# Loading block 0's values in long rows and gathering them on TensorE, in a chunked attention followed by a ReGLU feed-forward

## The chip, the cores and the metric

The kernel runs on one core of one Trainium2 chip. The time is device microseconds of one execution. Before the change it is 238.22 us, the median of 8 runs (237.99 to 238.51). A lower time is better.

## The reference

Attention over chunks of 32 queries: each chunk sees 8 memory rows, the 16 tokens to its left, its own 32 and the 8 to its right. The output is laid out as 3072 tokens of 512 numbers and goes through a gated feed-forward layer (FFN). `q`, `k`, `v` are 4 batches x 8 heads x 768 tokens x 64 in float32.

```
for c in range(nc):                                   # chunk 32, left 16, right 8
    l_start, r_end = max(0, c*32 - 16), min(S, c*32 + 32 + 8)
    k_full = concatenate([mem_k, k[:, :, l_start:r_end]], axis=2)
    v_full = concatenate([mem_v, v[:, :, l_start:r_end]], axis=2)
    scores = (1 / sqrt(64)) * q_c @ k_full.T
    a = softmax(scores)
    out[:, :, c*32:c*32+32] = a @ v_full
x = out.transpose(0, 2, 1, 3).reshape(3072, 512)
y = (maximum(x @ w_gate, 0) * (x @ w_val)) @ w_out    # 512 -> 1536 -> 512
```

## The kernel before

**Blocks and windows.** The tokens are worked in 8 blocks of 384 (`TB`), two for each batch. A block has four windows (`NQ`) of 96 queries; a window needs the 8 memory rows and 120 tokens (`BAND`), together 128 keys, one for each partition. Masks in the scores (block 0) or a bias in the exponential cut a window down to what each chunk of 32 sees. The eight heads go in four pairs, since two heads of 64 fill 128 partitions.

**Blocks 0 and 1.** They have nothing to hide behind and take a quicker way to their keys. `q` and `k` load in long rows: a partition holds four neighbouring tokens of a head (`J = 4`, 256 numbers). TensorE turns them (`turn_pe`, L199): for each of the four places in a row, `rk` is the stationary operand and a matrix of ones and zeros, `sel`, the moving one; this picks the rows that each window needs and transposes them in one step. `sel` for one window has 32 columns, 2 for the rows with the memory's eight tokens and 30 for the band's 120 tokens. `ident` does the same for the queries. In block 0 the result is written with a stride of four, so that tokens stand in their natural order. `turn_copy` (L210 to L216) brings it to SBUF in half precision on VectorE (DVE), the queries of pair 0 on ScalarE (ACT). `step_s0` (L250, L242, L254) makes the scores: a matmul with `maskk` and `maskq` writes the mask, eight add the products, and ACT takes the exponential. `wide_d` (L285) sums the exponentials with a matmul of ones, and ACT makes the reciprocal through a logarithm and an exponential (L288, L289). `ones[:, 1]` is for window 0 of block 0, whose 16 leftmost tokens don't exist. `wide_v` (L297) multiplies with the values `vwins` and DVE multiplies with the reciprocal (L299) into `xT`, the FFN's input.

**Values.** `vwins[p]` holds, for each window, the 8 memory rows and 120 band tokens of the eight heads in their key order. For block 0 `load_band` (L142) fetches the band with four DMAs, one a window, in rows of 64 numbers; the memory's rows come through `mem32`, are narrowed by DVE to `mem16` (L469) and copied into each window (L470).

**Queues.** Converting loads are issued by GpSimd (POOL), one after the other: block 0's keys and queries of heads 2 and 3, of heads 4 to 7, `ident` and `sel` between them (`select`, L429), the band of values, then the FFN's weights in slices of 256 columns (`load_w`, L172). [...] The keys and queries of heads 0 and 1 come in float32 through SP and ACT (`kst`, `qst`).

**FFN.** For each of 12 units of 128 columns `ffn_unit` (L342) makes gate and value with four matmuls each, ACT the positive part (L348), DVE the product `gv` (L349); `out_unit` (L368) multiplies `gv` with `wo`. Units 0 and 1 of block 0 are open together and are fed in `chunk`s, one for each head pair as it comes; unit 2 uses a spare double bank. The order of every engine is that of the program text; nothing reorders it.

**PSUM.** There are eight banks: `xo` and `xs`, and six that are first three double buffers (`tps`, for turns and scores of block 0), then four single ones (`fps`) and one double one (`sps`). `wide_v` of block 0 uses `xo` for all four pairs.

Of the kernel before, what the change touches and what calls it, by code (L numbers as in the profile page):

```python
# [17 lines left out]
def kernel(  # L18
# [12 lines left out]
    nc = tc.nc  # L31
# [52 lines left out]
    qbds = [const.tile([128, NQ, HP, 2, QB], F16, name=f"qbd{p}") for p in range(2)]  # L84
    memk, memv = (const.tile([NMEM, B * H, D], F16, name=nm) for nm in ("memk", "memv"))
    mem32 = const.tile([NMEM, H, D], F32, name="mem32")
    mem16 = const.tile([NMEM, H, D], F16, name="mem16")
    ones = const.tile([128, 3, D], F16, name="ones")
    bias = const.tile([128, 3], F32, name="bias")
    maskk = const.tile([128, 128], F16, name="maskk")  # L90
# [27 lines left out]
                       half.tile([QR, H, J * D], F16, tag="q16", name="rq"))  # L118
        return rows[n]

    def load_rows_mem(dma, dst, n, h0, nh):
        src = bass.AP(tensor=mem_k.tensor, offset=mem_k[n // 2, h0, 0, 0].offset,
                      ap=[[J * D, 2], [NMEM * D, nh], [1, J * D]])
        dma(dst, src)

    def load_k(n, h0, nh):
        pool_dma(rows_of(n)[0][0:KR, h0:h0 + nh], k_rows(n, h0, nh))  # L127
# [8 lines left out]
    def load_band(n, src_t, dsts):  # L136
        b, p = divmod(n, 2)
        for i in range(NQ):
            m0, m1 = (16 if (p == 0 and i == 0) else 0), (112 if (p == 1 and i == NQ - 1) else BAND)
            src = bass.AP(tensor=src_t.tensor, offset=src_t[b, 0, TB * p + QB * i - 16 + m0, 0].offset,  # L140
                          ap=[[D, m1 - m0], [S * D, H], [1, D]])
            pool_dma(dsts[p][NMEM + m0:NMEM + m1, i, :, 0:D], src)  # L142
# [38 lines left out]
        return pools["f"].tile([128, 512], F32, tag="f", name=name)  # L181

    def turn_pe(n, hp):

        if n != 1:
            pool, tag = (pools["t"], "t") if n == 0 else (pools["s"], "sc")
            ps = pool.tile([128, 2, 512], F32, tag=tag, name="kq_ps")
            kps, qps = ps[:, 0], ps[:, 1, 0:TB]
        else:
            ps, kps, qps = None, bank("k_ps"), bank("q_ps")[:, 0:TB]  # L190
        turns[n, hp] = ps, kps, qps
        rk, rq = (t.rearrange("p h (j d) -> p h j d", j=J) for t in rows_of(n))
        sel = sels[n % 2].rearrange("p i t -> p (i t)")

        for t, dst, w in ((rk, kps, sel[0:KR + 2]), (rq, qps, ident[:QR, :QR])):
            steps = dst.rearrange("p (r j) -> p j r", j=J) if n == 0 else dst.rearrange("p (j r) -> p j r", j=J)
            for j in range(J):
                for hh in range(2):
                    nc.tensor.matmul(steps[D * hh:D * hh + D, j], lhsT=t[:, 2 * hp + hh, j], rhs=w,  # L199
                                     start=True, stop=True)  # L200

    def turn_copy(n, hp):
        if n not in kTs:
            kq = turned.tile([128, HP, 512 + TB], F16, tag="kq", name="kq")
            kTs[n] = kq[:, :, 0:512].rearrange("p a (i m) -> p i a m", i=NQ)
            qTs[n] = kq[:, :, 512:].rearrange("p a (i m) -> p i a m", i=NQ)
            turns[n] = kq
        ps, kps, qps = turns.pop((n, hp))
        if n == 0 and hp == 0:
            dve_copy(turns[n][:, hp, 0:512], kps)  # L210
            act_copy(turns[n][:, hp, 512:], qps)
        elif n == 0:
            dve_copy(turns[n][:, hp], ps.rearrange("p a c -> p (a c)")[:, 0:512 + TB])
        else:
            for src, dst in ((kps, turns[n][:, hp, 0:512]), (qps, turns[n][:, hp, 512:])):
                dve_copy(dst.rearrange("p (r j) -> p r j", j=J), src.rearrange("p (j r) -> p r j", j=J))  # L216
# [19 lines left out]
    def score_mms(n, hp, sc, start):  # L236

        kT, qT = kTs[n], qTs[n]
        for i in range(NQ):
            for hh in range(2):  # L240
                s = slice(D * hh, D * hh + D)
                nc.tensor.matmul(sc[:, hh, QB * i:QB * i + QB], lhsT=kT[s, i, hp, :], rhs=qT[s, i, hp, :],  # L242
                                 start=start, stop=start or i == NQ - 1)

    def step_s0(n, hp):
# [43 lines left out]
        nc.scalar.activation(rinv, rinv, ACT.Exp, scale=-1.0, bias=mln64)  # L289
        rinvs[n, hp] = rinv  # L290

    def wide_v(n, hp):
        ex = exs.pop((n, hp))
        xo_ = xs if n == 1 and hp % 2 else xo
        for i in range(NQ):
            for hh in range(2):
                nc.tensor.matmul(xo_[D * hh:D * hh + D, QB * i:QB * i + QB], lhsT=vwins[n][:, i, 2 * hp + hh, 0:D],  # L297
                                 rhs=ex[:, hh, i, :], start=True, stop=True)
        nc.vector.tensor_tensor(out=x_of(n)[:, hp, :], in0=xo_, in1=rinvs.pop((n, hp)), op=ALU.mult)  # L299
# [45 lines left out]
    def ffn_close(n):  # L345
        for (g_ps, v_ps), m in units[n]:
            gr = grpool.tile([128, TB], F16, name="gr")
            nc.scalar.activation(gr, g_ps, ACT.Relu)  # L348
            nc.vector.tensor_tensor(out=gvs[n][:, m, :], in0=v_ps, in1=gr, op=ALU.mult)  # L349
# [37 lines left out]
    def fill(count):  # L387
        for i in range(count):
            nc.tensor.matmul(xo, lhsT=filler[:, 0:128], rhs=filler[:, 0:TB], start=True, stop=True)
# [9 lines left out]
    def words(t):  # L399
        return t.bitcast(U32)  # L400

    zero(words(filler), 0)
    zero(words(ident), 0)
    zero(words(sels[0].rearrange("p i t -> p (i t)")), 0)


    zero(vwins[0][0:NMEM + 16, 0, :, 0:D], 0.0)

    zero(words(maskk), 0)
    zero(words(maskq), 0)  # L410
    for g in range(3):
        r = slice(32 * g, 32 * g + 1)
        if g > 0:
            zero(maskk[r, NMEM:NMEM + 32 * g], NEG)
        if g < 2:
            zero(maskk[r, NMEM + 32 * g + 56:128], NEG)
        zero(maskq[r, 32 * g:32 * g + 32], 1.0)

    zero(words(ones.rearrange("p a d -> p (a d)")), 0x3C003C00)
    zero(ones[0:NMEM + 16, 1], 0.0)  # L420
    zero(ones[0:NMEM, 1], 1.0)
    zero(ones[96:128, 2], 0.0)
    zero(ones[96:120, 2], 1.0)
    zero(mln64, -LN64)
# [3 lines left out]
    def select(ap, fill_with, base, pattern, mult, op=ALU.not_equal):  # L428
        nc.gpsimd.affine_select(out=ap, in_=ap, compare_op=op, fill=fill_with, base=base, pattern=pattern,  # L429
                                channel_multiplier=mult)  # L430

    def build_sel(p):

        s = sels[p]
        first_row = -6 if p == 0 else 10
        parts = [(0, NQ, 2, 32)] if p == 0 else [(0, NQ, 2, 30), (0, NQ - 1, 30, 32)]
        for i0, i1, t0, t1 in parts:
            select(s[:, i0:i1, t0:t1], 1.0, -first_row - t0, [[-24, i1 - i0], [-1, t1 - t0]], 1)
        select(s[:, :, 0:2], 1.0, -KR, [[0, NQ], [-1, 2]], 1)

    load_k(0, 2, 2)
    load_rows_mem(pool_dma, rows_of(0)[0][KR:KR + 2, 2:H], 0, 2, H - 2)
    load_q(0, 2, 2)
    load_k(0, 4, 4)
    select(ident, 1.0, 0, [[-1, 128]], 1)
    build_sel(0)
    load_q(0, 4, 4)
    load_band(0, v, vwins)
    load_w(0, 256)
    load_w(256, 512)  # L450

# [11 lines left out]


    with tc.tile_pool(name="tps", bufs=3, space=bass.MemoryType.PSUM) as pools["t"]:
        fill(10)
        dve_copy(rows_of(0)[0][0:KR + 2, 0:2], kst)
        act_copy(rows_of(0)[1][:, 0:2], qst)
        dve_copy(mem16, mem32)  # L469
        mem_values = [lambda i=i: dve_copy(vwins[0][0:NMEM, i, :, 0:D], mem16) for i in range(NQ)]  # L470
        mem_values[0]()
        turn_pe(0, 0)
        turn_copy(0, 0)
        turn_pe(0, 1)
        turn_copy(0, 1)
        step_s0(0, 0)
        for i in range(1, NQ):
            mem_values[i]()
        turn_pe(0, 2)
        turn_copy(0, 2)  # L480
        step_s0(0, 1)
        wide_d(0, 0)
        turn_pe(0, 3)
        turn_copy(0, 3)
        step_s0(0, 2)
        wide_d(0, 1)
        step_s0(0, 3)
    pools["f"] = ctx.enter_context(tc.tile_pool(name="fps", bufs=4, space=bass.MemoryType.PSUM))
    pools["s"] = ctx.enter_context(tc.tile_pool(name="sps", bufs=1, space=bass.MemoryType.PSUM))
    wide_v(0, 0)  # L490
    wide_d(0, 2)
    wide_v(0, 1)
    zero(vwins[1][96:128, NQ - 1, :, 0:D], 0.0)


# [8 lines left out]
    select(bias, NEG, NMEM + 55, [[32, 3]], -1, ALU.is_ge)  # L504
    load_w(768, 1024)
    for i in range(NQ):
        nc.gpsimd.tensor_copy(vwins[1][0:NMEM, i, :, 0:D], mem16)
    load_w(1024, 1280)

    ffn_open(0, (0, 1))  # L510
    wide_v(0, 2)
    wide_d(0, 3)
    chunk(0, 0)
    chunk(0, 1)
    wide_v(0, 3)
    chunk(0, 2)
    chunk(0, 3)
    ffn_close(0)
    zero(words(k16s[0][0:32, 0].rearrange("p h d -> p (h d)")), 0)
    zero(words(k16s[1][96:128, NQ - 1].rearrange("p h d -> p (h d)")), 0)  # L520
    load_band(1, v, vwins)
# [5 lines left out]
    load_rows(2, 4, 4)  # L527

    ffn_unit(0, 2, spare=True)
    ffn_unit(0, 3)  # L530
    for hp in range(2):
        turn_pe(1, hp)
        turn_copy(1, hp)
    step_s(1, 0)
    for hp in range(2, HP):
        turn_pe(1, hp)
# [13 lines left out]
    ffn_unit(0, 8)  # L550
    ffn_unit(0, 9)
    for hp in range(HP):
        wide_v(1, hp)
    one_words(0, 0, NMEM + 16, 0, 1, 0)
    one_words(0, 0, NMEM, 0, 1, ONE)
    ffn_unit(0, 10)
# [88 lines left out]
```

The softmax here doesn't subtract the row's maximum and nothing guards it: scores larger than these inputs give would overflow.

## Time and profile before

| | |
|---|---|
| median of 8 runs | 238.22 us |
| the profiled execution | 238.51 us |
| its span, from the first to the last instruction | 236.6 us |
| TensorE busy, 0 to 40 us | 32.2 us |
| TensorE busy, 40 to 230 us | 190.0 us |
| first FFN matmul on block 0 (`g`; `v`) | 16.17; 17.31 us |
| first exponential of block 1 | 25.27 us |

The profile is of one execution and shows for each engine when each instruction ran and what released it. PE is TensorE's matmuls, PEld its weight loads. [...] a row's duration is longer than the distance to the next row; the distance is what counts. A DMA is shown by its issue on the queue, and its landing is given as a delay from there. In the table of stages the last three columns are TensorE's granted clock, the busy share of the 16 DMA engines, which sums overlapping packets and so exceeds 1, and GB/s.

### The profile page before, as it was taken

Reading aid. Unit: us, or ns where it says so; the run is one execution under the profiler, and the core shown is the slowest. Engines: PE = TensorE matmul, PEld = TensorE weight load, DVE = VectorE, ACT = ScalarE, POOL = GpSimd, SP = SyncE. Lnnn points to the kernel's source line nnn. Section 1 sums busy time; section 2 is a strip of 40 time slices with the busy share of each in tenths; the row PEclk is TensorE's granted clock in tenths of the full one; section 3 lists DMA queues with packets and bytes.
Section 4 is the critical chain, followed back from the end, with each engine's and each line's share of the span. In section 5 each row is a group of like instructions: output and inputs, shape, how many; then the busy total and the mean of one; then the engine's idle time right before and its main releaser. Section 6 shows DMA issues by size and latency. Waiting matters only on the chain.

```text
span 236.6 us, 4591 instructions
## 1 busy us (share of the span) xinstructions
PE 225.0 (95%) x1730; PEld 131.2 (55%) x1730; DVE 107.2 (45%) x215; ACT 141.0 (60%) x299; POOL 104.1 (44%) x131
## 2 busy tenths in 40 slices
PE   6869888999999999999999999999999999999993
PEld 3535545566544566546664666556664666455641
DVE  5655727889710155604642156405561266214400
ACT  3393693377752589728883599548881798433310
POOL 7988967945307940893099205960310000000000
PEclk9999999999999999999999999999999999999999
DMA  6999999999994999299939993999702100120012
GB/s 121 137 166 194 196 173 182 166 206 155 92 200 150 147 161 169 22 153 201 164 20 163 148 148 53 98 180 171 79 3 89 44 3 0 44 91 0 1 46 89
DMA packets 107324, 27.35 MB, mean 116 GB/s; under 512 B 91222, under 2 KB 104358, under 8 KB 107302
## 3 DMA queue, kind: packets, MB, share of 16 engines
q0 software_dynamic: 83008, 15.37, 80.7%
q1 hardware_dynamic: 20630, 5.33, 18.8%
q10 hardware_dynamic: 3664, 6.36, 7.8%
q8 instruction: 13, 0.21, 0.4%
q14 instruction: 9, 0.07, 0.1%
HBM read 31.15 MB, written 6.29 MB: 158 GB/s over the span
## 4 chain that ended last, share of the span: by engine, by line
PE 85%; DMA 4%; POOL 3%; ACT 3%; issue 2%; DVE 2%; POOLq 0%; DVEq 0%; ACTq 0%
PE g_ps L342 26%; PE v_ps L342 25%; PE o_ps L368 25%; DMA wv<-in_moe_w_val_dram 3%; PE sc_ps L267 3%; PE xo_ps L306 2%; ACT ex L273 2%; PE xs_ps L306 2%; POOL vwin L142 2%; PE kq_ps L199 1%; DMA out_dram<-o_sb 1%; PE sc_ps L242 1%; POOL rk L127 1%; PE gv_ps L342 1%; ACT rw L288 0%
## 5 line engine op out<-in xcount | busy, mean ns | idle before, releaser
L349 DVE TENSOR_TENSOR gv<-v_ps,gr 128x384 f16<-128x384 f32 x95 | 52.8, 557 | 97.4 <-ACT gr L348 84.2
L342 PE MATMUL v_ps<-xT,wv 128*128 128x384 f16 x380 | 78.3, 326 | 0.8 <-DMA wv<-in_moe_w_val_dram 0.8
L342 PE MATMUL g_ps<-xT,wg 128*128 128x384 f16 x380 | 78.3, 326 | 0.0
L368 PE MATMUL o_ps<-wo,gv 128*128 128x512 f16 x288 | 63.5, 379 | 0.0
L348 ACT ACTIVATE gr<-g_ps 128x384 f16<-128x384 f32 x95 | 46.0, 485 | 22.0 <-PE g_ps L342 10.8
L342 PEld LDWEIGHTS <-wg 128*128 128x128 f16 x384 | 36.6, 98 | 22.7
L342 PEld LDWEIGHTS <-wv 128*128 128x128 f16 x384 | 36.2, 98 | 22.8 <-DMA wv<-in_moe_w_val_dram 1.0
L368 PEld LDWEIGHTS <-gv 128*128 128x128 f16 x288 | 28.0, 98 | 33.0
L230 POOL COPY qbd<-qT 64x1536 f16<-64x1536 f16 x10 | 14.6, 1462 | 55.9 <-DMA qT<-q16n 55.6
L377 ACT COPY o_sb<-o_ps 128x512 f32<-128x512 f32 x23 | 13.5, 586 | 39.0 <-PE o_ps L368 31.0
L273 ACT ACTIVATE ex<-sc_ps,bias 128x256 f16<-128x256 f32 x84 | 33.3, 466 | 3.9 <-PE sc_ps L242 3.2
L142 POOL DMA_DIRECT2D vwin<-in_v_dram x32 | 29.1, 936 | 1.5 <-DMA memv<-in_mem_v_dram 1.1
L315 ACT ACTIVATE rinv<-ln,mln 64x768 f32<-64x768 f32 x24 | 22.1, 923 | 0.0
L310 ACT ACTIVATE ln<-xo_ps 64x384 f32<-64x384 f32 x24 | 11.7, 487 | 16.3 <-PE xs_ps L306 16.3
L168 POOL DMA_DIRECT2D q16n<-in_q_dram x20 | 15.6, 803 | 5.6 <-DMA wo<-in_moe_w_out_dram 5.6
L142 POOL DMA_DIRECT2D k<-in_k_dram x20 | 17.9, 910 | 0.0
L321 DVE TENSOR_TENSOR xT<-xo_ps,rinv 64x384 f16<-64x384 f32 x24 | 13.1, 547 | 10.0 <-ACT rinv L315 9.9
L321 DVE TENSOR_TENSOR xT<-xs_ps,rinv 64x384 f16<-64x384 f32 x24 | 13.2, 550 | 0.7
L306 PEld LDWEIGHTS <-vwin 128*128 128x128 f16 x192 | 10.6, 98 | 3.0
L310 ACT ACTIVATE ln<-xs_ps 64x384 f32<-64x384 f32 x24 | 11.4, 474 | 0.0
L306 PE MATMUL xo_ps<-ex,vwin 128*128 128x96 f16 x96 | 11.1, 206 | 0.0
L306 PE MATMUL xs_ps<-ex,vwin 128*128 128x96 f16 x96 | 11.1, 206 | 0.0
(79 smaller groups left out, 133.9 us busy)
## 6 DMA issues: line engine op xcount, KB each, us to landing
out_dram<-o_sb ACTq DMA_DIRECT2D x23, 256.0 KB
vwin<-in_v_dram POOLq DMA_DIRECT2D x24, 120.0 KB, 7.3
q16n<-in_q_dram POOLq DMA_DIRECT2D x20, 96.0 KB, 5.4
k<-in_k_dram POOLq DMA_DIRECT2D x15, 120.0 KB, 4.1
wg<-in_moe_w_gate_dram POOLq DMA_DIRECT2D x6, 256.0 KB, 7.6
wv<-in_moe_w_val_dram POOLq DMA_DIRECT2D x6, 256.0 KB, 8.1
wo<-in_moe_w_out_dram POOLq DMA_DIRECT2D x3, 512.0 KB, 10.8
rk<-in_k_dram POOLq DMA_DIRECT2D x5, 224.0 KB, 6.4
```

The source lines that it names most:

```text
L142: pool_dma(dsts[p][NMEM + m0:NMEM + m1, i, :, 0:D], src)
L168: pool_dma(q16s[n][:, i], src)
L230: nc.gpsimd.tensor_copy(qbds[n % 2][s, :, :, hh, :].rearrange("p i a m -> p (i a) m"), qTs[n][s].rearrange("p i a m -> p (i a) m"))
L273: nc.scalar.activation(flat[:, :, :, s], view[:, :, :, s], ACT.Exp, scale=SCALE, bias=bias[:, g:g + 1])
L306: nc.tensor.matmul((xo, xs)[hh][:, QB * i:QB * i + QB], lhsT=vw[:, i, 2 * hp + hh, :], rhs=ex[:, hh, i, :], start=True, stop=True)
L310: nc.scalar.activation(ln[:, hh], (xo, xs)[hh][D:128], ACT.Ln, scale=1.0 / 64.0)
L315: nc.scalar.activation(rinv, lns.pop((n, hp)), ACT.Exp, scale=-1.0, bias=mln64[0:D, :])
L321: nc.vector.tensor_tensor(out=x_of(n)[D * hh:D * hh + D, hp, :], in0=(xo, xs)[hh][0:D], in1=rinv[:, hh, :], op=ALU.mult)
L342: nc.tensor.matmul(ps[a], lhsT=(wg, wv)[a][:, f, 128 * m:128 * m + 128], rhs=xTs[n][:, f, :], start=(f == 0), stop=(f == NFC - 1))
L348: nc.scalar.activation(gr, g_ps, ACT.Relu)
L349: nc.vector.tensor_tensor(out=gvs[n][:, m, :], in0=v_ps, in1=gr, op=ALU.mult)
L368: nc.tensor.matmul(o_ps, lhsT=gvs[n][:, m, 128 * t:128 * t + 128], rhs=wo[:, m, :], start=(m == 0), stop=(m == NDC - 1))
```

## The change

Block 0's values come in long rows as its keys do: one DMA for 112 rows of 256 numbers for each head, and one for the memory's two rows, into a new tile `rv`. TensorE distributes them: `gather_v(i0)` makes, for two windows at a time, eight matmuls with `sel`'s 32 columns as stationary operand and `rv` at place `j` of the row as moving one; place `j` goes to the partitions 32 j to 32 j + 31. DVE copies the result, 128 x 1024, into `vwins[0]`. The keys of block 0 therefore stand by their place in the row: key 32 j + t is row t's token j. `turn_pe` writes them so, `maskk` is laid out so, and `ones[:, 1]` is made by four matmuls with `sel`.

Beside this: `ident` and `sel` are cleared by POOL and built before POOL's loads; the queries of pair 0 go through `xs` to a tile of their own, `q00`; the scores of pair 1 come ahead of the turn of pair 2; `wide_v` of pairs 1 and 3 uses a second double bank, `xo2`; the sums of pairs 2 and 3 are at other places; the turns of pairs 0 and 1 of block 1 come ahead of unit 3; clearing a part of `vwins[0]` moves from the start to after unit 1; one more filler matmul; `mem16` goes.

```diff
-        for t, dst, w in ((rk, kps, sel[0:KR + 2]), (rq, qps, ident[:QR, :QR])):
-            steps = dst.rearrange("p (r j) -> p j r", j=J) if n == 0 else dst.rearrange("p (j r) -> p j r", j=J)
+        ksteps, qsteps = (dst.rearrange("p (j r) -> p j r", j=J) for dst in (kps, qps))
+        if n == 0:
+            ksteps = kps.rearrange("p (i j t) -> p j i t", i=NQ, j=J)
+            qsteps = qps.rearrange("p (r j) -> p j r", j=J)
+        for t, steps, w in ((rk, ksteps, sel[0:KR + 2]), (rq, qsteps, ident[:QR, :QR])):
...
         if n == 0 and hp == 0:
             dve_copy(turns[n][:, hp, 0:512], kps)
-            act_copy(turns[n][:, hp, 512:], qps)
+            act_copy(q00, qps)
...
-    def wide_v(n, hp):
+    def wide_v(n, hp, xo_=xo):
...
-    zero(words(ident), 0)
-    zero(words(sels[0].rearrange("p i t -> p (i t)")), 0)
-    zero(vwins[0][0:NMEM + 16, 0, :, 0:D], 0.0)
...
+        keys = maskk[r].rearrange("p (j t) -> p j t", j=J)
         if g > 0:
-            zero(maskk[r, NMEM:NMEM + 32 * g], NEG)
+            zero(keys[:, :, 2:2 + 8 * g], NEG)
...
-    zero(ones[0:NMEM + 16, 1], 0.0)
-    zero(ones[0:NMEM, 1], 1.0)
...
+    nc.gpsimd.memset(words(ident), 0)
+    nc.gpsimd.memset(words(sels[0].rearrange("p i t -> p (i t)")), 0)
+    select(ident, 1.0, 0, [[-1, 128]], 1)
+    build_sel(0)
     load_k(0, 2, 2)
...
     load_k(0, 4, 4)
-    select(ident, 1.0, 0, [[-1, 128]], 1)
-    build_sel(0)
     load_q(0, 4, 4)
-    load_band(0, v, vwins)
+    pool_dma(rv[0:KR], bass.AP(tensor=v.tensor, offset=v[0, 0, 0, 0].offset,
+                               ap=[[J * D, KR], [S * D, H], [1, J * D]]))
+    load_rows_mem(pool_dma, rv[KR:KR + 2], 0, 0, H, mem_v)
     load_w(0, 256)
...
+        def gather_v(i0):
+
+            ps = pools["t"].tile([128, 2, 512], F32, tag="t", name="vg_ps")
+            for i in range(2):
+                for j in range(J):
+                    nc.tensor.matmul(ps[32 * j:32 * j + 32, i].rearrange("p (h d) -> p h d", h=H),
+                                     lhsT=sels[0][0:KR + 2, i0 + i, :], rhs=rv[:, :, D * j:D * j + D],
+                                     start=True, stop=True)
+            dve_copy(vwins[0][:, i0:i0 + 2, :, 0:D].rearrange("p i h d -> p (i h) d"),
+                     ps.rearrange("p i (h d) -> p (i h) d", h=H))
+
+        fill(11)
+
+        for j in range(J):
+            nc.tensor.matmul(xo[32 * j:32 * j + 32, 0:D], lhsT=sels[0][0:KR + 2, 0, :], rhs=ones[0:KR + 2, 0, :],
+                             start=True, stop=True)
...
-        dve_copy(mem16, mem32)
-        mem_values = [lambda i=i: dve_copy(vwins[0][0:NMEM, i, :, 0:D], mem16) for i in range(NQ)]
-        mem_values[0]()
+        dve_copy(ones[:, 1], xo[:, 0:D])
...
         step_s0(0, 0)
-        for i in range(1, NQ):
-            mem_values[i]()
+        step_s0(0, 1)
         turn_pe(0, 2)
         turn_copy(0, 2)
-        step_s0(0, 1)
         wide_d(0, 0)
...
         step_s0(0, 3)
+        gather_v(0)
+        wide_d(0, 2)
+        gather_v(2)
...
+    xo2 = pools["s"].tile([128, 2, 512], F32, tag="sc", name="xo2_ps")
     wide_v(0, 0)
-    wide_d(0, 2)
-    wide_v(0, 1)
+    wide_v(0, 1, xo2[:, 0, 0:TB])
...
     ffn_open(0, (0, 1))
+    wide_d(0, 3)
     wide_v(0, 2)
-    wide_d(0, 3)
     chunk(0, 0)
     chunk(0, 1)
-    wide_v(0, 3)
+    wide_v(0, 3, xo2[:, 1, 0:TB])
     chunk(0, 2)
     chunk(0, 3)
     ffn_close(0)
+
+    zero(vwins[0][0:NMEM + 16, 0, :, 0:D], 0.0)
...
     ffn_unit(0, 2, spare=True)
-    ffn_unit(0, 3)
     for hp in range(2):
         turn_pe(1, hp)
         turn_copy(1, hp)
+    ffn_unit(0, 3)
     step_s(1, 0)
```

More of the change, by code (lines that the diff above doesn't have):

```diff
@@ L86 @@
     mem32 = const.tile([NMEM, H, D], F32, name="mem32")
-    mem16 = const.tile([NMEM, H, D], F16, name="mem16")
+    rv = const.tile([KR + 2, H, J * D], F16, name="rv")
+    q00 = const.tile([128, TB], F16, name="q00")
     ones = const.tile([128, 3, D], F16, name="ones")
@@ L119, in rows_of, with load_rows_mem @@
         return rows[n]
-    def load_rows_mem(dma, dst, n, h0, nh):
-        src = bass.AP(tensor=mem_k.tensor, offset=mem_k[n // 2, h0, 0, 0].offset,
+    def load_rows_mem(dma, dst, n, h0, nh, src_t=mem_k):
+        src = bass.AP(tensor=src_t.tensor, offset=src_t[n // 2, h0, 0, 0].offset,
                       ap=[[J * D, 2], [NMEM * D, nh], [1, J * D]])
@@ L187, in turn_pe @@
             ps = pool.tile([128, 2, 512], F32, tag=tag, name="kq_ps")
-            kps, qps = ps[:, 0], ps[:, 1, 0:TB]
+            kps, qps = ps[:, 0], xs if (n, hp) == (0, 0) else ps[:, 1, 0:TB]
         else:
@@ L241, in score_mms @@
                 s = slice(D * hh, D * hh + D)
-                nc.tensor.matmul(sc[:, hh, QB * i:QB * i + QB], lhsT=kT[s, i, hp, :], rhs=qT[s, i, hp, :],
+                rhs = q00[s, QB * i:QB * i + QB] if (n, hp) == (0, 0) else qT[s, i, hp, :]
+                nc.tensor.matmul(sc[:, hh, QB * i:QB * i + QB], lhsT=kT[s, i, hp, :], rhs=rhs,
                                  start=start, stop=start or i == NQ - 1)
@@ L290, in wide_d @@
         rinvs[n, hp] = rinv
-    def wide_v(n, hp):
+    def wide_v(n, hp, xo_=xo):
         ex = exs.pop((n, hp))
-        xo_ = xs if n == 1 and hp % 2 else xo
         for i in range(NQ):
@@ L412 @@
         r = slice(32 * g, 32 * g + 1)
+        keys = maskk[r].rearrange("p (j t) -> p j t", j=J)
         if g > 0:
-            zero(maskk[r, NMEM:NMEM + 32 * g], NEG)
+            zero(keys[:, :, 2:2 + 8 * g], NEG)
         if g < 2:
-            zero(maskk[r, NMEM + 32 * g + 56:128], NEG)
+            zero(keys[:, :, 2 + 8 * g + 14:32], NEG)
         zero(maskq[r, 32 * g:32 * g + 32], 1.0)
     zero(words(ones.rearrange("p a d -> p (a d)")), 0x3C003C00)
-    zero(ones[0:NMEM + 16, 1], 0.0)
-    zero(ones[0:NMEM, 1], 1.0)
     zero(ones[96:128, 2], 0.0)
@@ L465 @@
     with tc.tile_pool(name="tps", bufs=3, space=bass.MemoryType.PSUM) as pools["t"]:
-        fill(10)
+        def gather_v(i0):
[11 more added lines that the diff above has]
+                             start=True, stop=True)
         dve_copy(rows_of(0)[0][0:KR + 2, 0:2], kst)
         act_copy(rows_of(0)[1][:, 0:2], qst)
-        dve_copy(mem16, mem32)
-        mem_values = [lambda i=i: dve_copy(vwins[0][0:NMEM, i, :, 0:D], mem16) for i in range(NQ)]
-        mem_values[0]()
+        dve_copy(ones[:, 1], xo[:, 0:D])
         turn_pe(0, 0)
@@ L506 @@
     for i in range(NQ):
-        nc.gpsimd.tensor_copy(vwins[1][0:NMEM, i, :, 0:D], mem16)
+        nc.gpsimd.tensor_copy(vwins[1][0:NMEM, i, :, 0:D], mem32)
     load_w(1024, 1280)
     ffn_open(0, (0, 1))
+    wide_d(0, 3)
     wide_v(0, 2)
-    wide_d(0, 3)
     chunk(0, 0)
     chunk(0, 1)
-    wide_v(0, 3)
+    wide_v(0, 3, xo2[:, 1, 0:TB])
     chunk(0, 2)
@@ L552 @@
     for hp in range(HP):
-        wide_v(1, hp)
+        wide_v(1, hp, (xo, xs)[hp % 2])
     one_words(0, 0, NMEM + 16, 0, 1, 0)
```

## The prediction, made before the changed kernel ran

> **What bounds the kernel now.** I read the page's busy shares, then the busy time by stage, then what TensorE waited for, then the chain of waits of the first 50 us, last single rows of the timeline.
>
> ```profile
> span 236.6 us, 4591 instructions
> PE 225.0 (95%) x1730; PEld 131.2 (55%) x1730; DVE 107.2 (45%) x215; ACT 141.0 (60%) x299; POOL 104.1 (44%) x131
> ```
>
> ```profile
> 5.00:10.00 5.00, 3.49 (x58) 2.57 (x57) 3.31 (x7) 1.45 (x3) 5.00 (x7) 1.00 1.36 130
> 10.00:15.00 5.00, 4.63 (x78) 2.63 (x75) 2.74 (x3) 4.03 (x7) 5.00 (x10) 1.00 1.67 150
> 15.00:20.00 5.00, 3.49 (x35) 1.87 (x35) 1.95 (x4) 2.31 (x6) 3.46 (x7) 1.00 1.40 184
> 40.00:230.00 190.00, 190.00 (x1332) 110.93 (x1331) 84.33 (x155) 117.56 (x252) 70.60 (x76) 1.00 1.03 106
> ```
>
> The columns of the second fence are stage, length, then busy us of PE, PEld, DVE, ACT, POOL. From 40 us to 230 us TensorE is never idle, so nothing there can be won by this change: the time is decided by how early TensorE enters that stage. What the first 40 us leave idle is named by the waits (engine, line, releaser, us in total, times, longest):
>
> ```profile
> PE xo_ps L297 <- DVE xT L299: 1.8, 3, 0.7
> PE kq_ps L199 <- DMA rq<-in_q_dram: 0.8, 1, 0.8
> PE kq_ps L199 <- POOL sel L429: 0.8, 1, 0.8
> PE v_ps L342 <- DMA wv<-in_moe_w_val_dram: 0.8, 1, 0.8
> PE sc_ps L242 <- DVE kq L216: 0.7, 1, 0.7
> ```
>
> The chain (start, us, what) shows which of them ends last:
>
> ```profile
> 5.98 3.71 POOL vwin L142 x4
> ...
> 10.47 6.79 DMA wv<-in_moe_w_val_dram
> 17.26 0.05 issue
> 17.31 0.34 PE v_ps L342
> ...
> 23.15 0.56 DVE gv L349
> 23.71 1.07 DVE kq L216 x2
> 24.78 0.04 issue
> 24.82 0.36 PE sc_ps L242 x8
> 25.22 0.05 issue
> 25.27 1.21 ACT ex L273 x3
> ```
>
> The reader is to see two things. First, four issues of the value load keep POOL for 3.71 us ahead of the weights, and the FFN's first `v` matmul waits until 17.31 for them, though attention's first output was ready at about 14.6. Second, the FFN's work leads through unit 3's product and two copies to block 1's first exponentials at 25.27; from there ACT sets the pace until TensorE is full at 33.6 us. So I reckon the start of those exponentials: its shift is the shift of the end.
>
> ```profile
> 9.64 0.52 PE L199 MATMUL kq_ps<-ident,rq 96*64 96x96 f16 x8 [0.83 <-DMA rq<-in_q_dram]
> ...
> 10.20 1.09 DVE L213 CAST kq<-kq_ps 128x896 f16<-128x896 f32 x1 [0.98 <-PE kq_ps L199]
> ...
> 11.96 1.09 DVE L213 CAST kq<-kq_ps 128x896 f16<-128x896 f32 x1 [0.67 <-PE kq_ps L199]
> ```
>
> These rows show the other path that counts: heads 4 to 7 of block 0's queries land, TensorE turns them, DVE copies twice 1.09 us.
>
> [...] The trace has no 32-column matmul[...]: eight of 96 columns at L297 let the next row begin 0.16 us later (13.55 to 13.71). [...] 512 columns in 0.69 us and 896 in 1.09 make 1.04 ns a column. [...] 135 GB/s between 9 and 11 us, where the packets are the values' 128 B, 178 to 196 GB/s from 13 to 20 us with 512 B packets. [...] POOL's selections would now stand beside DVE's memsets, in the trace they stand beside two casts, so I price them as they are.
>
> **The change, part by part.** Times below are on the clock of the profile.
>
> *POOL.* Now: four DMA issues from 1.35, the three selections 4.26 to 5.33, queries of heads 4 to 7 issued at 5.28, values 5.97 to 9.69, weights from 9.68. After: two memsets and the selections come first. POOL may start at about 0.8 (SP and ACT issue at 0.80). A memset of 64 words isn't in the trace for POOL; its memsets of one column last 0.10, DVE's of 64 words 0.11; I take 0.1 each, 0.3 at most, not below nothing since DVE's own come free only in slack. With 0.1 for waits and 1.07 for the selections, the first load is issued at 2.2 (bound 2.6) instead of 1.35. Then 0.82 + 0.61 + 0.67 + 0.75 put the last query load at 5.05, against 5.28. The value load: four issues of 0.93 (3.72) become one, priced as the nearest row of 120 x 8 rows (0.93), and one of 0.62 for the memory's two rows: the weights are issued at 7.3 instead of 9.68.
>
> *Landing.* Keys of heads 4 to 7 took 4.8 us from issue, queries 4.3, landing 1.39 after each other. Issued at 4.3 and 5.05: by its own delay the query load lands at 9.35, behind the keys with the old distance at 10.5. I take 9.85 (before 9.58). Both ends go into the range. The first turns also wait: pair 1's queries land at 3.63 + 3.3 = 6.9 instead of 6.07, but the scores of pair 1 now come ahead of the turn of pair 2, so this lies beside the same wait and costs nothing unless the late load comes sooner.
>
> *Values.* 459 kB of 512 B packets at 178 GB/s: 2.6 us, landed at 12.45; at 135 GB/s 3.4, at 13.25. Then the four weight loads at 1.35 each (17.26, 18.61, 19.95 landed at this distance): the first `wv` at about 15.2. The 0.8 us wait for it goes; what is late next is the gather.
>
> *Attention's front.* Queries at 9.85, first copy 0.56 later: 10.41 to 11.5, second to 12.6. Now the scores of pair 3 follow that copy's end by 0.23 (13.05 to 13.28) and take 0.28: the gather starts at 13.1, after its rows have landed. It is 2 x 8 matmuls of 512 columns. o_ps shows 0.216 each (54 in 11.65), in fours beside each other 0.43 for eight, alone 1.73; I take 0.43, plus 0.2 until DVE may start. DVE's copies are 1024 columns: 1.04 x 1024 + 0.16 = 1.22 each. First 13.75 to 14.97, second to 16.2; TensorE's second half of the gather hides under the first copy. Then the second half of wide_v and the product: 16.6 to 17.16. wide_v of pair 2 must wait for it (same bank), then 0.29: `g` begins at 17.5. Now `v` begins at 17.31 with one `g` already done. From 17.31 to wide_v of pair 3 it is 1.24 for seven matmuls, so 1.40 for eight; from there to unit 2 1.73 (18.55 to 20.28). Unit 2 begins at 20.63 instead of 20.28: **0.35 later**. The second bank for pairs 1 and 3 removes two of the three L297 waits, but they lay before the weights' landing and are paid again by the copies.
>
> *Units 2 and 3 and the turns.* Unit 3 moves behind two turns. Now unit 2 starts t = 20.28 and the exponentials t + 4.99. After: unit 2's product can start at t + 2.02 as now (22.30), but a third memset of 0.27 stands before it in DVE's queue; the two there already end 0.14 before the product, and each needs 0.36 with its gap. So the product is 0.24 late. Then 0.56, k copy 0.68, q copy 0.55 (t + 4.05); unit 3 must wait for them, as its two banks are those just turned into; its `v` ends at about t + 4.85 and the exponentials begin at t + 5.25. The 0.7 us wait of the scores at L242 is not won, it becomes a wait of unit 3: **0.25 later**. Queued behind unit 3's `g` are the scores of pair 0, and ACT waits for those.
>
> *At nothing:* copying the query turn to its own tile by ACT, mask memsets in 3-d, the extra fill, the four matmuls and the copy for the ones (all before 5.9, under the wait for the loads; without it 0.3 to 0.5, from 64 columns at 1.04 ns with their fixed part and four short matmuls); unstrided key writes, perhaps 0.1 a turn, under DVE's copies; the value memory's rows no longer copied by DVE (0.51 and four of 0.27, 1.6 us in all, which lay beside waits of DVE for TensorE).
>
> **Sum:** 0.35 + 0.25 = 0.6. The profiled execution is 238.51 us (span 236.6 and 1.9 around it), so 239.1; it was the slowest of eight whose median is 238.22. Against the median: **238.8 us**.
>
> **The rivals.** *Early loads (not slower).* Now the late keys and queries are issued on either side of the selections; after, in one run. If the last queries land with the 3.3 to 3.4 us that the small loads need instead of 4.3 to 4.8, at 8.4 to 9.2, then everything from DVE's first copy to unit 2 is 0.65 to 1.5 earlier; at 8.85 this is 1.0, so 237.8. It decides from a landing at 9.25 (238.2). For it: between 7 and 8 us the DMA engines moved only 94 GB/s. Against it: keys now start 0.9 later and the queries follow them on the same queue. *Gather one by one (slower).* If four column groups don't run together, DVE's second copy starts 1.73 + 0.28 + 1.73 + 0.2 = 3.94 after the gather's begin instead of 1.89: 2.05 more, 240.9. Against it: the 64-column rows. *Rows late (slower; the change doesn't do what it says).* If the long rows go no faster than the short, they land 13.25 to 14.1, and TensorE waits in the gather: 0.2 to 1.0 more, 239.5 at 0.7. Against it: the 178 to 196 GB/s.
>
> **How the numbers follow.** Forecast 0.43 (own range 238.3 to 239.3), early loads 0.32, one by one 0.10, rows late 0.15. A measurement of this kernel tells 0.2% (0.48 us) from no change. Faster comes from three quarters of the early loads: 0.24. Within 0.2%: the rest of these, 0.08, and 0.16 of the forecast's low part: 0.24. Slower: 0.27 of the forecast and both slow rivals: 0.52. The range, 237.4 to 240.1, leaves out the lowest part of the early loads and the one-by-one case. The likeliest case gives the time.
>
> **What would show it.** Right: the last query load lands at 9.4 to 10.5; no wait for `wv`; a TensorE wait for the copies of vg_ps of 1.5 us or more before wide_v; two copies of about 1.22; unit 3's `g` waiting for the kq copies; the exponentials of block 1 beginning 0.3 to 1.0 after 25.27. Wrong: queries landed by 9.25; copies well under 1.1; eight gather matmuls taking over 1 us; TensorE falling back to 0.33 us for 384 columns, as its fillers at the start show, in the idle stretch before the FFN.

## The result, and the profile after

The changed kernel takes 241.04 us in the median of 11 executions (239.23 to 242.06), the kernel before 238.24 (31 executions beside it, 237.77 to 239.03). The ratio is 1.0111, 95% interval 1.0095 to 1.0127: slower, and by more than the range of the prediction allowed. The profiled execution took 241.49 us with a span of 239.3, so 2.2 us lie around it.

The head of the page, and TensorE's clock in 40 slices:

```profile
span 239.3 us, 4626 instructions
PE 228.1 (95%) x1751; PEld 131.7 (55%) x1751; DVE 107.7 (45%) x209; ACT 141.2 (59%) x299; POOL 101.6 (42%) x131
...
PEclk9797999999999999999999999999999999999999
```

TensorE is busy for 3.1 us more than before (228.1 against 225.0), though the gather adds only sixteen matmuls in two groups of 0.6 us. The last row says why: the second and the fourth slice stand at 7 tenths. Between the two, and after them, the clock is full. Cut at the places where the clock changes, the stages look like this (stage, length, busy us of PE, PEld, DVE, ACT and POOL with their instructions, then the granted clock, the DMA share and GB/s):

```profile
4.17:7.58 3.41, 2.21 (x39) 1.32 (x37) 1.35 (x3) 1.10 (x2) 3.41 (x6) 1.00 1.12 132
7.58:10.99 3.41, 3.41 (x42) 1.72 (x38) 1.09 (x1) 1.58 (x2) 3.41 (x8) 0.50 1.26 152
10.99:14.40 3.41, 3.37 (x62) 1.78 (x58) 2.10 (x3) 2.68 (x6) 1.52 (x3) 1.00 1.41 185
14.40:17.82 3.42, 1.67 (x34) 0.72 (x33) 2.98 (x4) 2.33 (x5) 2.15 (x4) 1.00 1.44 191
17.82:21.23 3.41, 3.41 (x24) 1.66 (x23) 1.23 (x3) 0.74 (x2) 3.18 (x8) 0.50 1.45 195
21.23:24.60 3.37, 3.37 (x38) 1.94 (x36) 2.11 (x5) 1.18 (x3) 3.37 (x6) 1.00 1.45 196
```

Two stretches of 3.41 us run at half clock, and each follows a stretch of the same length in which TensorE stood idle for a good part: it was busy for 2.21 us of 3.41 ahead of the first, 1.67 of 3.42 ahead of the second, where its longest wait was 0.86. The two half-clock stretches were full (3.41 busy), and the full clock follows each of them. The clock changes at 7.58, 10.99, 17.82 and 21.23 us and falls again at 239.68, behind the last instruction. The distances are 3.41, 6.83, 3.41 and 218.45 us: 1, 2, 1 and 64 steps of 3.413. In the profile of the kernel before the clock stays full from 4.39 us to 236.5, after TensorE's last matmul, which is 232.11 us or 68 such steps. Counted back from that fall in these steps, the emptiest of its stretches up to 230 us is this one:

```profile
14.63:18.04 3.41, 1.89 (x26) 1.11 (x26) 1.39 (x3) 2.68 (x5) 2.53 (x4) 1.00 1.38 178
```

1.89 us busy kept the clock there; 1.67 and 2.21 lost it here. The count depends on where a stretch is taken to begin: from 13.95 to 17.36, off these steps, TensorE of the kernel before is busy for only 1.53 us, and the clock stayed. With 1.89 us, between the two, the kernel before is close to losing it too.

The waits of TensorE in the first 42 us (what waited, for what; us in total, times, longest) show what took the place of the wait for `wv`, which is gone:

```profile
PE xo_ps L301 <- DVE vwin L476: 1.4, 2, 0.9
...
PE xo_ps L301 <- DVE xT L303: 1.1, 2, 0.7
PE g_ps L346 <- DVE kq L220: 1.0, 1, 1.0
PE kq_ps L203 <- DMA rq<-in_q_dram: 1.0, 1, 1.0
```

The first is the wait for the copies of the gathered values, the third that of unit 3 for the query turns; both were foreseen, the first at 1.5 us or more. The chain of waits from the gather to block 1's first exponentials (start, us, what):

```profile
13.79 0.57 PE vg_ps L473 x8
14.37 0.02 issue
14.39 2.37 DVE vwin L476 x2
16.76 0.04 issue
16.80 0.29 PE xo_ps L301 x4
...
17.19 0.57 DVE xT L303
17.76 0.04 issue
17.80 0.53 PE xo_ps L301 x8
18.33 0.43 PE g_ps L346
18.77 0.32 PE v_ps L346
19.09 0.32 PE g_ps L346
...
20.69 0.32 PE v_ps L346
21.01 0.41 PE xo_ps L301 x8
21.42 0.27 PE g_ps L346
21.69 0.16 PE v_ps L346
...
28.02 1.21 ACT ex L278 x3
```

One FFN matmul after another takes 0.32 us up to 21.0 and 0.16 us from 21.69 on: the same instruction, on either side of the end of the second stretch. The exponentials begin at 28.02 instead of 25.27, 2.75 us later; the span is 2.7 us longer. As the prediction assumed, their shift is the shift of the end. The question is what the 2.75 us consist of.

### The profile page after: what moved, and what is told of

Its sections match the earlier page's. It is cut to its first block, busy times and chain, and to the rows that moved or that the text cites. A ratio compares the mean times of both kernels' runs of the same rounds, so it can differ in the third digit from the quotient of the medians.

```text
span 239.3 us, 4626 instructions
## 1 busy us (share of the span) xinstructions
PE 228.1 (95%) x1751; PEld 131.7 (55%) x1751; DVE 107.7 (45%) x209; ACT 141.2 (59%) x299; POOL 101.6 (42%) x131
## 4 chain that ended last, share of the span: by engine, by line
PE 87%; ACT 3%; DVE 3%; DMA 2%; issue 1%; POOL 1%; POOLq 0%; DVEq 0%; ACTq 0%
PE g_ps L346 26%; PE v_ps L346 25%; PE o_ps L372 25%; PE sc_ps L272 3%; PE xo_ps L310 2%; PE kq_ps L203 2%; ACT ex L278 2%; PE xs_ps L310 2%; DMA rq<-in_q_dram 2%; PE sc_ps L247 1%; DVE vwin L476 1%; PE sc_ps L255 1%; DMA out_dram<-o_sb 1%; DVE gv L353 1%; DVE xT L303 1%
## 5 line engine op out<-in xcount | busy, mean ns | idle before, releaser
L346 PE MATMUL g_ps<-xT,wg 128*128 128x384 f16 x380 | 79.1, 328 | 1.0 <-DVE kq L220 1.0
L346 PE MATMUL v_ps<-xT,wv 128*128 128x384 f16 x380 | 79.1, 328 | 0.0
L143 POOL DMA_DIRECT2D vwin<-in_v_dram x28 | 25.3, 934 | 1.9 <-DMA memv<-in_mem_v_dram 1.9
L325 DVE TENSOR_TENSOR xT<-xo_ps,rinv 64x384 f16<-64x384 f32 x24 | 13.1, 547 | 10.0 <-ACT rinv L319 9.9
```

Of the source, the lines that this page charges most:

```text
L325: nc.vector.tensor_tensor(out=x_of(n)[D * hh:D * hh + D, hp, :], in0=(xo, xs)[hh][0:D], in1=rinv[:, hh, :], op=ALU.mult)
L346: nc.tensor.matmul(ps[a], lhsT=(wg, wv)[a][:, f, 128 * m:128 * m + 128], rhs=xTs[n][:, f, :], start=(f == 0), stop=(f == NFC - 1))
```

## The experiments

Theory: the loss has two parts. The gather and its copies cost about 1 us with TensorE at full clock; the rest is the half clock, which falls because TensorE now waits for two copies of DVE just ahead of the FFN. Rivals: that the half clock only slows work which was late anyway, so that filling the gaps brings nothing; that the order of unit 3 and the turns is what costs; that the early selections on POOL bring or cost the time by themselves.

Medians of all runs, with the number of executions whose mean granted clock over the span was at least 0.995. Those have no half-clock stretch that weighs; a mean near 0.993 is one stretch, 0.986 two, as in the profile above. The counts include the profiled execution. The ratios are estimates of their own and differ from the quotients of the medians by up to 0.3%.

| Kernel | median us | ratio to before (95%) | at full clock |
|---|---|---|---|
| changed kernel | 241.04 | 1.0111 (1.0095 to 1.0127) | 2 of 12 |
| e1: fillers in both gaps | 239.62 | 1.0040 (1.0016 to 1.0064) | 11 of 11 |
| e2: filler at the gather alone | 239.62 | 1.0054 (1.0037 to 1.0071) | 11 of 15 |
| e3: filler at the turns alone | 240.25 | 1.0082 (1.0054 to 1.0110) | 4 of 8 |
| e4: e1, unit 3 at its old place | 239.55 | 1.0049 (1.0026 to 1.0072) | 10 of 11 |
| e5: before, TensorE kept idle | 242.73 | 1.0163 (1.0121 to 1.0205) | 0 of 4 |
| e6: e5, the gap filled | 240.04 | 1.0071 (1.0051 to 1.0092) | 8 of 8 |
| e7: before, selections first | 238.50 | 0.9998 (0.9971 to 1.0025) | 8 of 12 |
| e8: e1, gather by heads | 238.64 | 1.0012 (0.9996 to 1.0027) | 12 of 12 |
| e9: e1, a memset later | 239.57 | 1.0044 (1.0026 to 1.0062) | 19 of 20 |
| e10: e1 without the gather | 238.59 | 1.0005 (0.9989 to 1.0022) | 19 of 20 |
| e11: e8, the second half behind pair 1 | 238.62 | 0.9995 (0.9974 to 1.0017) | 19 of 20 |

The kernel before, run beside each set, kept the full clock in 30 of 36, 24 of 27 and 45 of 55 executions, with medians of 238.39, 238.15 and 238.31 us among these. The others took about 240.

**Fillers in the two gaps (e1 to e3).** The fillers are matmuls of zeros into a bank that nobody reads yet, as the kernel has them at its start.

```
         turn_copy(0, 0)
+        fill(5)             # e1, e3
         turn_pe(0, 1)
...
         gather_v(2)
+        fill(8)             # e1, e2
```

> The changed kernel with filler matmuls in TensorE's two idle stretches: five between the turns of pairs 0 and 1, eight after the second half of the gather. Clock theory: the two stretches at half the TensorE clock vanish (mean clock 1.000), first exponential of block 1 near 25.9 us instead of 28.0, time 238.9 (238.5 to 239.3). Rival, the gather and its copies cost the time by themselves: filler work changes nothing or adds to it, 241 or more.

> Only the eight fillers after the gather. Clock theory: the half-clock stretch before 11 us stays (clock 0.993), the one at 18 to 21 us goes; 0.6 us later than with both fillings: 239.5. Rival: 241.

> Only the five fillers between the turns of pairs 0 and 1. Clock theory: the stretch before 11 us goes, the one at 18 to 21 us stays (clock 0.993); eight FFN matmuls at 0.32 instead of 0.16 us cost 1.3 and the rest 0.2: 240.4. Rival: 241.

With both, all eleven executions keep the full clock and the time falls by 1.4 us, to the 239.62 that lies between the two executions of the changed kernel (239.23 and 239.89) which kept it by themselves. That is 0.7 us above the 238.9 that was expected of it. Adding matmuls made the kernel faster: the half clock isn't hidden behind waits. The filler at the gather does most of it. In e2 the first half-clock stretch was expected to stay, yet 11 of 15 executions keep the full clock; e3 lost it in half of its executions, at 241.13 in the median against 239.81 for the other half. In e1's timeline (start, busy us, engine, line, what; in brackets the idle time before and its releaser):

```profile
13.37 0.61 PE L473 MATMUL vg_ps<-rv,sel 114*32 114x512 f16 x8 [0.23 <-DMA rv<-in_mem_v_dram]
14.03 2.36 DVE L476 CAST vwin<-vg_ps 128x1024 f16<-128x1024 f32 x2 [1.29 <-PE vg_ps L473]
...
17.73 0.34 PE L346 MATMUL g_ps<-xT,wg 128*128 128x384 f16 x1
...
26.11 1.20 ACT L278 ACTIVATE ex<-sc_ps,bias 128x256 f16<-128x256 f32 x3 [0.50 <-PE sc_ps L247]
```

This is the changed kernel at the clock that the prediction priced: `g` at 17.73 (forecast 17.5), exponentials at 26.11 (forecast 25.87). The difference of 0.24 is nearly all the gather's wait of 0.23 for its rows, the first line, which the changed kernel's own profile doesn't show since its scores, at half clock, came later than the rows.

**The order of unit 3 (e4).**

```
     ffn_unit(0, 2, spare=True)
+    ffn_unit(0, 3)
     for hp in range(2):
         turn_pe(1, hp)
         turn_copy(1, hp)
-    ffn_unit(0, 3)
```

> Both fillings, and unit 3 of block 0 back ahead of the turns of block 1. My account says that the new order only moves a wait from the scores to unit 3, so the same as with both fillings within 0.1 us: 238.9. Rival, the new order is worth the 0.7 us wait it removes: 0.5 us or more slower than with both fillings, 239.5. Third reading, the new order costs time through the banks that unit 3 waits for: 0.3 us faster, 238.6.

239.55 against 239.62: no difference. The wait only changes its place, from the scores to unit 3, as was reckoned.

**Idleness alone (e5, e6).** Three memsets of an unused tile hold DVE where the copies of the gather stand in the changed kernel; the kernel is otherwise that of before. e6 fills TensorE's gap.

```
+    for _ in range(3):
+        zero(scratch, 0.0)
     wide_v(0, 0)
     wide_d(0, 2)
+    fill(10, spare)         # e6
     wide_v(0, 1)
+    fill(3, spare)          # e6
```

> The kernel before with three memsets of 128x1024 on DVE (0.91 us each) ahead of the first product of wide_v, which then starts near 15.8 instead of 14.0 us: TensorE idles longer, and no other part of the change is in it. Clock theory: TensorE's clock halves for one 3.41 us stretch after it in most runs (0.993), 240.5; in a run at full clock 239.0. Rival, the clock has to do with something else in the changed kernel (the 32-column matmuls, the longer DMA rows): clock 0.996 to 1.000 nearly always as before, 239.0.

> As e5_before_idle with 13 filler matmuls in the idle TensorE time that the memsets make. Clock theory: clock 0.996 to 1.000, 239.0. Rival: same time as e5_before_idle.

By stage, with the columns as above, e5:

```profile
14.00:16.00 2.00, 0.33 (x4) 0.13 (x4) 1.44 (x3) 1.97 (x4) 1.83 (x3) 1.00 1.29 171
16.00:18.00 2.00, 0.36 (x8) 0.23 (x8) 1.48 (x3) 0.30 (x1) 0.78 (x2) 1.00 1.46 193
18.00:20.00 2.00, 1.88 (x18) 1.07 (x18) 0.90 (x3) 1.10 (x2) 1.43 (x3) 0.72 1.45 193
20.00:22.00 2.00, 2.00 (x14) 0.82 (x13) 0.36 (x1) 0.00 (x0) 1.78 (x5) 0.50 1.45 196
```

and e6:

```profile
16.00:18.00 2.00, 2.00 (x20) 1.10 (x19) 1.32 (x2) 0.76 (x2) 1.12 (x2) 1.00 1.45 192
18.00:20.00 2.00, 1.88 (x21) 1.11 (x20) 1.39 (x3) 0.79 (x2) 1.30 (x5) 1.00 1.45 193
20.00:22.00 2.00, 2.00 (x19) 1.02 (x17) 0.56 (x1) 0.40 (x2) 1.92 (x4) 1.00 1.45 195
```

In e5 TensorE works 0.69 us of the four from 14 to 18, and from 18.9 to 22 the clock is 0.50. In e6 it is 1.00 throughout and the time is 2.7 us lower, with the same delay on DVE. So the half clock needs nothing of the gather: a DVE delay ahead of the FFN is enough, and filling takes it back. Both came later than expected. e6 is 1.0 us above, since the memsets followed each other at 1.19 us and held the product up (to 16.49 in e5, where 15.8 was reckoned). e5 is 2.2 above: three of its four executions have a mean clock of 0.986, as two half-clock stretches give, where one was expected.

**POOL's selections first (e7)**, with the value load left in its four parts:

```
-    zero(words(ident), 0)
-    zero(words(sels[0].rearrange("p i t -> p (i t)")), 0)
...
+    nc.gpsimd.memset(words(ident), 0)
+    nc.gpsimd.memset(words(sels[0].rearrange("p i t -> p (i t)")), 0)
+    select(ident, 1.0, 0, [[-1, 128]], 1)
+    build_sel(0)
     load_k(0, 2, 2)
...
-    select(ident, 1.0, 0, [[-1, 128]], 1)
-    build_sel(0)
     load_q(0, 4, 4)
```

> The kernel before with one part of the change: POOL clears and builds ident and sel ahead of its loads. My account: the last query load lands as before (9.6), the first one 0.9 us later, which lies under the same wait: 238.4 at full clock, with a half-clock stretch before 11 us in some runs, median 238.6. Rival, the early selections win the 0.8 us wait for sel: 237.7.

238.50, ratio 0.9998 (0.9971 to 1.0025): by itself this part wins and costs nothing that can be told, which here means 0.6 us. It lost the full clock in 4 of 12 executions, against 3 of 27 of the kernel before beside it, too few to tell apart. In its profile the clock is 0.50 from 10.84 to 14.25 us, after a stretch in which TensorE was busy for 1.90: neither the gather nor the long rows of values are needed for that either.

**What the gather costs (e10).** e10 leaves out the gather and the copies; block 0's values are zero in it, and fillers stand in TensorE's place.

```
-        gather_v(0)
+        fill(4)
         wide_d(0, 2)
-        gather_v(2)
         fill(8)
```

> Both fillings, the two halves of the gather with their copies left out (block 0's values are then zero, and its attention output with them), four fillers in place of the first half. My account: wide_v starts after pair 3's scores and the FFN is then held by the weights' landing near 16.1 us instead of the copies' end near 16.4 and the products after it, so unit 2 begins about 1.5 us sooner: 238.1. Rival, the gather is hidden behind the weights: 239.4 or more.

```profile
14.07 1.47 PE L393 MATMUL xo_ps<-filler 128*128 128x384 f16 x8
15.47 0.53 PE L301 MATMUL xo_ps<-ex,vwin 128*64 128x96 f16 x16
15.95 1.02 DVE L303 TENSOR_TENSOR xT<-xo_ps,rw 128x384 f16<-128x384 f32 x2 [3.25 <-PE xo_ps L301]
16.85 0.34 PE L346 MATMUL g_ps<-xT,wg 128*128 128x384 f16 x1
...
25.22 1.20 ACT L278 ACTIVATE ex<-sc_ps,bias 128x256 f16<-128x256 f32 x3 [0.50 <-PE sc_ps L247]
```

The exponentials begin at 25.22 against e1's 26.11, and the median falls by 1.03 us (by the two ratios 0.8): at full clock the gather and its copies cost 0.8 to 1.0 us more than the fillers in their place. And with these the kernel just equals the one before (25.27; ratio 1.0005). That isn't yet the bound of what the change could win, for the twelve fillers stand in the path themselves: the scores of pair 3 are followed by fillers from 13.03 on, and wide_v begins at 15.47 behind them, with no wait of TensorE between. The next to hold the FFN would be the weights: `wv` landed at 7.42 + 9.3 = 16.7, so `v`, which began at 17.02, could have come 0.3 us sooner at most in this execution. There was little to be won behind the value load: these weights, issued 3 us earlier than in the kernel before, landed only 0.5 us earlier. What an idle gap in place of the fillers would do to the clock isn't shown.

**Three tries at a version that beats both (e8, e9, e11).** e8 gathers four heads at a time, so that pairs 0 and 1 need only the first copy; e11 besides puts the second half behind wide_v of pairs 0 and 1; e9 moves a memset of DVE out of the way of unit 2's product.

```
-        step_s0(0, 3)
         gather_v(0)            # e8, e11: heads 0 to 3, 256 columns a matmul
+        step_s0(0, 3)
         wide_d(0, 2)
-        gather_v(2)
+        gather_v(4)            # e8: here; e11: after wide_v(0, 1)
...
-    zero(vwins[0][0:NMEM + 16, 0, :, 0:D], 0.0)
...
     ffn_unit(0, 7)
+    zero(vwins[0][0:NMEM + 16, 0, :, 0:D], 0.0)     # e8, e9, e11
```

> The changed kernel with both fillings, the gather split by heads instead of windows (so pairs 0 and 1 can start after DVE's first copy), its rows loaded in two DMAs of four heads, the first half of the gather ahead of pair 3's scores, and the clearing of vwins moved 10 us later. My account of the chain (gather, copies, product one after the other): unit 2 begins near 19.5 instead of 20.3 us and the exponentials of block 1 near 24.6: 237.6 at full clock, faster than both kernels. Rival, the weights' landing at 16.1 us or the rows' landing at 13.4 sets the FFN's start: 238.4 to 239.

> The changed kernel with both fillings and the clearing of a part of vwins[0] moved from ahead of unit 2's product to after unit 7. My account: the product of unit 2 starts 0.24 us sooner and so do the exponentials of block 1: 239.3 to 239.4 against 239.6. Rival, the memset lies in slack: 239.6.

> As e8_by_heads, and the second half of the gather comes after the products of pairs 0 and 1, in a bank of its own, so that these wait for DVE's first copy alone; pair 3's output in that bank; fillers for the rest. My account: first product near 15.2 us, the FFN's start then set by the weights' landing near 16.2, unit 2 near 19.8 instead of 20.78: 237.7, faster than both kernels. Rival, the weights land later or the second copy holds pair 2: 238.4 to 238.8, no gain over the kernel before.

e9's exponentials begin 0.23 us before e1's, 0.06 of which it had before unit 2; the medians differ by 0.05, so this stays undecided. e8 is 1.0 us below e1, e11 the same (by the ratios 0.7 and 1.1), and both equal the kernel before, where 237.6 and 237.7 were expected. What brought e8's gain isn't shown: it changes several things at once, and in its profile `g` begins at 17.64, only 0.09 us before e1's. There wide_v begins at 16.27, behind the eight fillers, though the first copy had ended at 14.66 and `wv` landed at 15.8. Timeline of e11:

```profile
15.38 1.02 DVE L303 TENSOR_TENSOR xT<-xo_ps,rw 128x384 f16<-128x384 f32 x2 [0.71 <-PE xo_ps L301]
16.03 0.66 PE L393 MATMUL spare_ps<-filler 128*128 128x384 f16 x3
16.32 1.22 DVE L476 CAST vwin<-vg_ps 128x1024 f16<-128x1024 f32 x1
16.91 0.34 PE L346 MATMUL g_ps<-xT,wg 128*128 128x384 f16 x1
...
19.39 0.32 PE L346 MATMUL g_ps<-xT,wg 128*128 128x384 f16 x1 [0.55 <-DVE xT L303]
```

The products come 1.45 us before e1's, yet `g` begins only 0.8 us earlier: from 15.47 to 16.9 TensorE makes the second half of the gather, three fillers and the sums of pair 3, while `wv` had landed at 15.9. The matmuls of pair 2's product stand behind the chunks of pairs 0 and 1 here, so that product comes late: 0.55 us of wait in the middle of the FFN. In the profiles of both runs it is the fillers and the order of TensorE's work that hold the FFN's start, not the weights. None of these runs beats the kernel before.

## Why the prediction was wrong

The side was right (slower, 0.52), the size not: 238.8 forecast, 241.04 measured, outside 237.4 to 240.1. By its own steps:

- **POOL's front: right within 0.5.** The first load is issued at 1.79 (forecast 2.2), the last queries at 4.58 (5.05). The two selections took 0.47 instead of the 0.83 they were priced at.
- **Landing of the last queries: right.** 4.58 + 5.1 = 9.7, forecast 9.85. The rival of early loads (by 9.25) fell.
- **First turns: put at nothing, and it cost time.** Pair 1's queries landed at 3.22 + 4.0 = 7.2 (forecast 6.9, before 6.03). TensorE waited 1.0 us for them, was busy for only 2.21 us of the stretch from 4.17 to 7.58, and ran the next stretch at half clock; this is worth 0.35 us in the sum below.
- **Rows: the late bound, but not shown to be for the rival's reason.** The values landed at 5.24 + 7.9 = 13.1, the memory's rows at 6.06 + 7.3 = 13.36; forecast 12.45, late bound 13.25. From 9.65 to 13.10 us the DMA engines moved 172 GB/s, near the 178 of the forecast, and in the kernel before 130. But they moved 0.59 MB in that time, of which the values are at most 459 kB; the forecast gave the values all of it. At full clock the late rows cost 0.23 to 0.27 us (e1), not the rival's 0.7.
- **Weights: the wait is gone, the landing gained less.** `wv` landed at 7.39 + 8.7 = 16.1, forecast 15.2; 17.26 before. In e1 and e10 it was 16.8 and 16.7.
- **Gather and copies: right.** Eight 32-column matmuls led to DVE's start in 0.67 us (14.39 less 13.72; forecast 0.63, one by one 1.93), so they do run beside each other and the rival "one by one" fell. The forecast's 0.43 for eight was an estimate: four beside each other, at the 0.216 us that the profile before shows for one of 512 columns. The copies took 1.18 each, forecast 1.22.
- **From unit 2 to the exponentials: right.** 5.23 us, forecast 5.25, before 4.99; unit 3 waits 1.0 us for the turns.
- **The eight FFN matmuls from `g` to wide_v of pair 3: the step that failed.** Forecast 1.40 us, measured 2.67 (18.27 to 20.94 in the timeline). They were priced at 0.16 us each, the spacing of before; in the profile they follow each other at 0.32.
- **Two readings were loose**, without weight in the sum. From 15 to 16 us the kernel before moved 157 GB/s, below the 178 to 196 given for 13 to 20. And the row at 13.71 is a weight load; but behind the same eight matmuls (`wide_v`, 128 x 64 weights, 96 columns each) at 15.72 a matmul does begin at 15.88, 0.16 us later.

The failed assumption is wider than that one term: every TensorE duration was priced at the full clock, while the same text put a wait of two copies, 2.4 us, into TensorE's path ahead of the FFN. Clock loss stood last among the signs of error; it should have been a rival with a chance and a price. The miss of the exponentials, 28.02 against 25.87, divides so: the gather starts 0.62 late, of which 0.27 are the rows (e1: 13.37 against 13.1) and 0.35 the first half-clock stretch (13.72 against 13.37); 0.15 more up to `g`; 1.27 in the eight matmuls; 0.12 from there to unit 2: together 2.16 of 2.15 us.

That this is the cause is shown, not only read: e1 takes the half clock away and gives 239.62, inside the range; e5 brings it about without the gather, e6 takes it back. What is left at full clock is 0.84 us by the exponentials where 0.6 was forecast, and 1.0 by the ratio or 1.2 by the medians (239.62 against 238.39 of the kernel before beside it, at full clock); the profiled execution of before (238.51) lay above its median and that of e1 (239.45) below its own.

Open is how little work of TensorE makes the clock fall. The thirteen profiled executions narrow it down, each cut into stretches of 3.41 us from the changes of clock in its own trace. Seven stretches ahead of 20 us were followed by half clock: TensorE was busy in them for 1.12 us (e5), 1.65 (e2), 1.67 and 2.21 (changed kernel), 1.83 (e4), 1.90 (e7) and 1.95 (e3). Of those between the first full clock and 230 us that kept it, one held 1.89 (kernel before), all others 2.28 or more. So the busy time of the stretch before tells nearly, but not wholly, what the clock does. The changes lie at other times in each execution (4.39 us in the kernel before, 7.58 in the changed kernel, 10.84 in e7, 18.9 in e5; against the steps of the changed kernel 0.2 us late, 0, 0.15 early, 1.1 late), and from one execution to the next the same kernel keeps or loses the clock. So these stretches don't begin at a fixed time from the kernel's start, and no run here set where they begin.

## What to carry to other kernels

Before a wait is put into TensorE's path, count how much TensorE works in the 3.4 us around it; where that falls towards two thirds or less (here half clock followed upon 1.12 to 2.21 us), price the following 3.4 us at half clock too, and try a few matmuls of zeros in the gap, which here brought back 1.4 of 2.8 us; then look whether they hold up the work behind them, as they do in e8, e10 and e11. Don't carry the gain at a load's issue over to its landing unmeasured: `wv`, issued 3.1 us earlier, landed 1.2 us earlier, in e1 and e10 only 0.4 and 0.5. And leave the new work out altogether early on: where that only equals the kernel before, as here, see what holds that run (fillers in e10, and 0.3 us behind them the weights) before a cheaper form of the work is tried.

## What was unexpected in the hardware

- TensorE's clock was halved for 3.41 us after a stretch in which it had been busy for half (1.67 us of 3.42) or even two thirds (2.21 of 3.41) of the time.
- The kernel before, too, fell below a mean clock of 0.995 in 19 of 118 executions, at a cost of about 1.6 us.
- The same two selections took 0.83 us on POOL where they stood beside DVE's casts from fp32, and 0.47 us where only memsets ran on DVE; the cause wasn't tested. In the timelines of before and of after:

```profile
4.50 0.83 POOL L429 TENSOR_SCALAR_AFFINE_SELECT sel<-sel 128x120 f16<-128x120 f16 x2
```

```profile
1.37 0.47 POOL L427 TENSOR_SCALAR_AFFINE_SELECT sel<-sel 128x120 f16<-128x120 f16 x2
```

- From 9.65 to 13.10 us the DMA engines moved 172 GB/s in the changed kernel, where 1156 of 1305 packets have 512 B or more, and 130 in the kernel before, where most are smaller (2343 of 2351 from 9 to 11 us). From 14.40 to 24.60 the changed kernel moved 191 to 196.
